# Pads between the four weight tables of a banded attention and feed-forward kernel

## The chip, the cores and the metric

The kernel runs on one core of a Trainium2 chip. The metric is the device time of one execution in microseconds. A core has several engines that run their own instruction streams: TensorE (PE in the profile, its weight loads PEld), VectorE (DVE), ScalarE (ACT), GpSimd (POOL) and SyncE (SP), which here issues DMAs. They work on SBUF, a memory of 128 partitions, and on PSUM, into which TensorE writes its products.

## The reference

Attention over a band of 64 keys, eight heads of 64 in each of eight sequences of 576, and behind it two dense layers with a leaky rectifier between them:

```python
scores = scale * np.matmul(q, k.transpose(0, 1, 3, 2))
mask = (rel >= 0) & (rel < window)          # window = 64
attn = softmax(np.where(mask, scores, -1000000000.0))
x = np.matmul(attn, v)                      # as (4608, 512)
h = x @ w_in                                # (512, 2048)
g = np.maximum(h, 0.0) + alpha * np.minimum(h, 0.0)
return (g @ w_out).astype(np.float32)       # (2048, 512)
```

The weights come as 64-bit numbers; the kernel converts them itself.

## The kernel before

The 4608 rows are 36 tiles of 128, taken in 9 blocks of 4. Attention of a tile leaves x, transposed, as the sum of two float32r tiles: xh, the rounded value, and xl, the rest. Each weight is held as such a sum too, in four tables of 128 partitions: `win_h`, `win_l`, `wout_h`, `wout_l`. They are made in lines 317 to 393, from raw pieces that SyncE fetches. For each block a loop runs over f from 0 to 15 (16 groups of 128 hidden units). A cell (one f of one block) has these steps:

- `hidden` (line 606): h, 128 units by 512 rows, is the sum of 12 products: win_h with xh, win_h with xl, win_l with xh, each over 4 chunks c. The stationary operand, loaded into TensorE ahead of the product, is a 128x128 piece of the weight table, the moving one 512 columns of xh or xl.
- `slopes`, `most`, `high`, `rest` (lines 612 to 630): ScalarE and VectorE apply the rectifier, ScalarE rounds to gh, and GpSimd takes the rest as gl (VectorE in block 0).
- `outs` (line 644): for each of the 4 tiles three products add to the output: gh with wout_h, gh with wout_l, gl with wout_h. Here a 128x128 piece of gh or gl is stationary, and 512 columns of the table move. Output tiles are copied out and stored at f = 15.

In block 0 the first four f are done in two halves of 256 rows.

The tables hold f from 0 to 11. What belongs to f from 12 to 15 lies in rooms of another pool, sb, that loads of q, k and v use first (`LATE`, line 214; `weight`, line 285, finds the place).

TensorE also computes the scores (s, line 466), the transposes of the probabilities (t, line 529, with the tile ident) for the first 8 tiles, their products with v (av, line 565), and idle products (spare, line 304, with one tile as both operands) that fill its waits at the start.

The order of all work is made by a planner in lines 51 to 206: each step is given engines and durations written in the code, 300 random trials with a fixed seed look for a good order, and the instructions are issued in it.

Where a tile lies in SBUF follows from the order in which the pools hand out room. The pool const begins with masks (1024 bytes in a partition), ident (512), alpha_sb (512), three tiles of 64 and six of 32 bytes; then come the four tables, xh and xl (16,384 bytes each) and pt_0. The pool sb comes behind it.

Of the kernel before, what the change touches and what calls it, by code (L numbers as in the profile page):

```python
# [10 lines left out]
F32 = mybir.dt.float32  # L11
# [39 lines left out]
class Plan:  # L51
# [144 lines left out]
    def fill(self, done):  # L196
# [14 lines left out]
NBLK = 4  # L211
PAIRS = 4

LATE = (("wout_h", 12, "z0"), ("wout_h", 14, "z1"), ("wout_l", 12, "z2"), ("wout_l", 14, "z3"),
        ("win_h", 12, "z4"), ("win_h", 14, "z5"), ("win_l", 12, "z6"), ("win_l", 14, "z7"))
ROOMS = {0: ("q", "k", "z0"), 1: ("q", "k", "z1"), 2: ("z4", "z5", "z2"), 3: ("z6", "z7", "z3")}
# [7 lines left out]
def banded_attention_then_prelu_ffn(  # L224
# [12 lines left out]
    P = 128  # L237
# [16 lines left out]
    const = ctx.enter_context(tc.tile_pool(name="const", bufs=1))  # L254
# [21 lines left out]

    stats = [[const.tile([P, NH], F32, name=f"{x}{i}") for x in ("nm", "sm", "rc")] for i in range(2)]


    parts_of = {}  # L280
    for name in ("win_h", "win_l", "wout_h", "wout_l"):
        ends = sorted(f for n, f, _ in LATE if n == name)
        parts_of[name] = {0: const.tile([P, ends[0], E], F32R, name=name)}

    def weight(name, f):
        f0 = max(x for x in parts_of[name] if x <= f)
        return parts_of[name][f0][:, f - f0, :]
# [8 lines left out]
    stock.update({f"x{i}": [i] for i in range(RING)})  # L296
    for _, _, z in LATE:
        stock[z], stock["late " + z] = [z], []
# [18 lines left out]
    def weights(c):  # L317
# [46 lines left out]
        def late(part):  # L364
            return [Buffer("late " + z, 1) for n, f0, z in LATE if (n, f0) == (name + part, f)]

        def begin(part):
            for n, f0, z in LATE:
                if (n, f0) == (name + part, f):
                    f1 = min([x for m, x, _ in LATE if m == n and x > f0], default=NF)  # L370
                    parts_of[n][f0] = sb.tile([P, f1 - f0, E], F32R, tag=z, name=f"{n}_{f0}")
# [365 lines left out]
    for n in range(2, NB + 1):  # L737
        for i in (0, 1):
            m, f = (n - 1, STAYS[1]) if i else (n - 2, STAYS[0]) if n > 2 else (1, 1)
            stays[m, f] = [n * NBLK + 2 * i, n * NBLK + 2 * i + 1] if n < NB else []  # L740
    for n in range(NB):
        ts = list(range(n * NBLK, (n + 1) * NBLK))
        if n < 2:
            for i, t in enumerate(ts):
                if n == 0:
                    _, _, st_done[t] = attend(t, True, EARLY[i])
                else:
                    f = 4 * i - 4 * (i == 3) // 3
# [69 lines left out]
```

## Time and profile before

| what | value |
|---|---|
| median of 3 runs | 896.2 us |
| lowest, highest | 895.82, 896.66 us |
| profiled execution | 895.07 us |
| its span | 893.3 us |
| ScalarE rescaling h (line 612) | 688 ns each |
| GpSimd taking gl (line 629) | 1290 ns each |

The span is the time from the first to the last instruction of the profiled execution; the execution's own time is 1.8 us longer. "Busy" is the time in which an engine has at least one instruction under way. A matmul's duration in the profile reaches from its start to its modelled end, and the next one starts before that end, so the pace of TensorE is read from the distance between starts.

### The profile page before, as it was taken

The page shows a single profiled execution, that of the slowest core. Times are in us where ns is not written, and L with a number is a line of the kernel's source. Part 1 is how long each engine was busy: PE and PEld are TensorE (multiplying, and loading weights), DVE is VectorE, ACT ScalarE, POOL GpSimd, SP SyncE. Part 2 cuts the span into 40 slices and gives each one's busy share as a digit, 9 for nine tenths or more (in the row PEclk, how much of TensorE's full clock was granted, in tenths as well). Part 3 has the DMA queues.
Part 4 walks back from the last instruction along what each step waited for, and adds up shares of the span by engine and source line. Part 5 has one row for each costly group of instructions (what it writes and reads, how often), then busy time and mean ns, then how long its engine had stood idle before and what let it go on. Part 6 is the DMA issues. An engine that isn't in the chain of part 4 may idle for free.

```text
span 893.3 us, 15479 instructions
## 1 busy us (share of the span) xinstructions
PE 885.7 (99%) x5951; PEld 733.9 (82%) x5951; DVE 429.2 (48%) x1319; ACT 380.6 (43%) x1022; POOL 307.6 (34%) x240
## 2 busy tenths in 40 slices
PE   8999999999999999999999999999999999999998
PEld 8888788888888888888888888888888888888886
DVE  6889863762726181716344362627171726311111
ACT  7988755433334262524352433335152524222222
POOL 5777842332313232323131332314142323121221
PEclk9999999999999999999999999999999999999999
DMA  8766643122203050303130212104030311001001
GB/s 308 238 229 192 194 129 107 28 79 51 105 17 91 1 153 2 107 1 107 48 107 1 80 75 51 56 13 142 1 107 1 107 47 49 1 1 48 1 0 49
DMA packets 55387, 69.70 MB, mean 78 GB/s; under 512 B 3456, under 2 KB 48784, under 8 KB 55312
## 3 DMA queue, kind: packets, MB, share of 16 engines
q1 hardware_dynamic: 54576, 68.04, 24.3%
q8 instruction: 47, 0.77, 0.4%
q10 hardware_dynamic: 736, 0.66, 0.2%
q14 instruction: 28, 0.23, 0.1%
HBM read 59.25 MB, written 9.44 MB: 77 GB/s over the span
## 4 chain that ended last, share of the span: by engine, by line
PE 93%; ACT 2%; DMA 2%; DVE 1%; POOL 1%; issue 0%; ACTq 0%; POOLq 0%; SPq 0%; DVEq 0%
PE h L606 43%; PE o L644 42%; PE s L466 4%; PE av L565 4%; DMA raw<-w_out 1%; ACT w L495 1%; DMA q<-qT 1%; POOL val L360 0%; PE t L529 0%; PE spare L304 0%; ACT g L612 0%; DVE val L356 0%; ACT win_h L375 0%; ACT wout_h L375 0%; ACT xh L569 0%
## 5 line engine op out<-in xcount | busy, mean ns | idle before, releaser
L629 POOL TENSOR_TENSOR gl<-g,gh 128x512 fp32r<-128x512 f32 x128 | 165.1, 1290 | 385.2 <-PE o L644 246.1
L619 DVE SCALAR_TENSOR_TENSOR g<-h,s_sb,g 128x512 f32<-128x512 f32 x128 | 96.1, 751 | 292.1 <-ACT g L612 292.0
L644 PE MATMUL o<-wout_h,gh 128*128 128x512 f32 x576 | 225.3, 391 | 0.0
L644 PE MATMUL o<-wout_l,gh 128*128 128x512 f32 x576 | 224.4, 390 | 0.3 <-DVE wout_l L379 0.3
L612 ACT ACTIVATE g<-h,sa_sb 128x512 f32<-128x512 f32 (+1 forms) x148 | 100.1, 676 | 227.2 <-PE h L606 199.8
L495 ACT ACTIVATE w<-w,nm 128x128 f32<-128x128 f32 x288 | 112.2, 393 | 114.0 <-DVE nm L489 113.9
L644 PE MATMUL o<-wout_h,gl 128*128 128x512 f32 x576 | 159.0, 389 | 0.0
L606 PE MATMUL h<-xh,win_h 128*128 128x512 f32 (+1 forms) x592 | 157.7, 388 | 0.6 <-ACT gh L625 0.4
L606 PE MATMUL h<-xl,win_h 128*128 128x512 f32 (+1 forms) x592 | 155.0, 384 | 0.0
L606 PE MATMUL h<-xh,win_l 128*128 128x512 f32 (+1 forms) x592 | 155.0, 384 | 0.0
L550 DVE STREAM_TRANSPOSE pt<-w 32x256 f32<-32x256 f32 x336 | 141.4, 430 | 6.3 <-POOL w L512 2.1
L625 ACT CAST gh<-g 128x512 fp32r<-128x512 f32 x128 | 79.4, 620 | 133.1 <-DVE g L619 83.9
L606 PEld LDWEIGHTS h<-xh,win_h 128*128 128x128 f32 x592 | 108.1, 188 | 24.7 <-issue 2.4
L512 POOL TENSOR_TENSOR w<-w,rc 128x1024 f32<-128x1024 f32 (+1 forms) x44 | 70.1, 1593 | 168.7 <-DVE rc L508 167.9
L606 PEld LDWEIGHTS h<-xl,win_h 128*128 128x128 f32 x592 | 109.5, 188 | 22.2
L606 PEld LDWEIGHTS h<-xh,win_l 128*128 128x128 f32 x592 | 109.5, 188 | 22.2
L644 PEld LDWEIGHTS o<-wout_h,gh 128*128 128x128 f32 x576 | 108.1, 188 | 22.9 <-issue 0.5
L644 PEld LDWEIGHTS o<-wout_l,gh 128*128 128x128 f32 x576 | 108.2, 188 | 22.7 <-DVE wout_l L379 0.6
L644 PEld LDWEIGHTS o<-wout_h,gl 128*128 128x128 f32 x576 | 108.1, 188 | 22.6
L489 DVE CUSTOM_DVE_ANT_0 w<-s,masks 128x128 f32<-128x128 f32 x288 | 63.8, 286 | 123.4 <-PE s L466 123.4
L495 ACT ACTIVATION_READ_ACCUMULATOR w<-w,nm 128x1 f32 x288 | 54.8, 190 | 0.0
L360 POOL TENSOR_TENSOR val<-val,low 128x512 int32<-128x512 int32 x32 | 41.0, 1290 | 11.8 <-DVE val L356 7.5
(52 smaller groups left out, 490.5 us busy)
## 6 DMA issues: line engine op xcount, KB each, us to landing
v<-vN SPq DMA_DIRECT2D x72, 256.0 KB, 4.5
k<-kT SPq DMA_DIRECT2D x35, 384.0 KB, 5.7
out<-os SPq DMA_DIRECT2D x35, 256.0 KB, 2.2
q<-qT SPq DMA_DIRECT2D x34, 256.0 KB, 5.7
raw<-w_in SPq DMA_DIRECT2D x16, 512.0 KB, 4.5
raw<-w_out SPq DMA_DIRECT2D x16, 512.0 KB, 4.2
k<-kT SPq DMA_DIRECT2D x2, 192.0 KB, 3.2
q<-qT ACTq DMA_DIRECT2D x2, 128.0 KB, 3.4
```

What stands on the lines that cost most here:

```text
L360: nc.gpsimd.tensor_tensor(out=d["val"], in0=d["val"], in1=d["tail"], op=ALU.add)
L466: nc.tensor.matmul(some[x][h * W:(h + 1) * W, u, y - ys.start], q[r, y, h, u * W:(u + 1) * W], k[r, y, u:u + 2, h, :], start=True, stop=True)
L489: nc.vector.tensor_tensor_reduce(out=w, in0=s, in1=m, op0=ALU.add, op1=ALU.min, scale=-SCALE, scalar=3.0e38, accum_out=d["nm"][:, g:g + 1])
L495: nc.scalar.activation(w, w, AF.Exp, scale=-1.0, bias=d["nm"][:, g:g + 1], accum_out=d["sm"][:, g:g + 1])
L512: nc.gpsimd.tensor_tensor(out=w, in0=w, in1=d["rc"][:, g].unsqueeze(2).broadcast_to(list(w.shape)), op=ALU.mult)
L550: nc.vector.transpose(d["pt"][ks, :, r], d["w"][r, :, ks])
L606: nc.tensor.matmul(ph[:, :nt], weight(wt, f)[:, c * P:(c + 1) * P], xt[:, c, xs], start=(k == 0), stop=(k == 3 * NP - 1))
L612: nc.scalar.activation(d["g"], d["h"][:, :nt], AF.Copy, scale=sa_sb[:, f:f + 1])
L619: nc.vector.scalar_tensor_tensor(out=g, in0=d["h"][:, :nt], scalar=s_sb[:, f:f + 1], in1=d["g"], op0=ALU.mult, op1=ALU.max)
L625: nc.scalar.copy(d["gh"], d["g"])
L629: (nc.vector if start else nc.gpsimd).tensor_tensor(out=d["gl"], in0=d["g"], in1=d["gh"].bitcast(F32), op=ALU.subtract)
L644: nc.tensor.matmul(po[t], gt[:, i * P:(i + 1) * P], weight(wt, f), start=(f == 0 and k == 0), stop=(f == NF - 1 and k == 2))
```

## The change

Three tiles without use are allocated in the pool const: 16 floats behind win_h, 16 behind win_l and 32 behind wout_h. A float has four bytes, so the pads have 64, 64 and 128 bytes in each partition.

```diff
+SHIFTS = {"win_h": 16, "win_l": 16, "wout_h": 32}
+
...
     parts_of = {}
     for name in ("win_h", "win_l", "wout_h", "wout_l"):
         ends = sorted(f for n, f, _ in LATE if n == name)
         parts_of[name] = {0: const.tile([P, ends[0], E], F32R, name=name)}
+        if name in SHIFTS:
+            const.tile([P, SHIFTS[name]], F32, name=f"pad_{name}")
```

Everything allocated behind a pad is moved by it. Counted within a line of 512 bytes, win_l starts 64 bytes further on than win_h, wout_h 128, and wout_l, xh, xl, pt_0 and the pool sb 256.

## The prediction

> **What bounds the kernel now.** I read the page's busy table first, then its chain, to learn which engine sets the end.
>
> ```profile
> span 893.3 us, 15479 instructions
> PE 885.7 (99%) x5951; PEld 733.9 (82%) x5951; DVE 429.2 (48%) x1319; ACT 380.6 (43%) x1022; POOL 307.6 (34%) x240
> ...
> PE 93%; ACT 2%; DMA 2%; DVE 1%; POOL 1%; issue 0%; ACTq 0%; POOLq 0%; SPq 0%; DVEq 0%
> ```
>
> TensorE is busy 99% of the span, and 93% of the chain that ended last is TensorE work. Matmuls overlap, though, so a busy TensorE can still lose time between two starts. The chain in order of time shows how fast the starts follow each other:
>
> ```profile
> 190.68 10.88 PE h L606 x48
> 201.56 13.60 PE o L644 x60
> ...
> 775.99 13.60 PE o L644 x60
> ```
>
> Each piece is a start, a duration and a count. 10.88 / 48 and 13.60 / 60 are both 0.2267 us: one product with 512 columns every 226.7 ns, for h and for o alike, early and late in the run. Nothing but the product itself sets that pace, as the waits of TensorE show. These are its longest:
>
> ```profile
> PE spare L304 <- DVE xl L303: 1.1, 1, 1.1
> PE s L466 <- DMA q<-qT: 1.1, 1, 1.1
> PE av L565 <- DVE pt L536: 0.5, 1, 0.5
> PE h L606 <- ACT gh L625: 0.4, 1, 0.4
> ```
>
> Three microseconds among them. The throttle is no cause either; the mean clock is in the row of the core:
>
> ```profile
> core 0: 893.3 us, clock 0.999
> ```
>
> Next I ask how much of the 226.7 ns is columns and how much comes once per product. The first four f of block 0 are done in halves of 256 columns; the timeline of TensorE alone has them:
>
> ```profile
> 21.41 0.64 PE L606 MATMUL h<-xl,win_h 128*128 128x256 f32 x4
> 21.89 0.64 PE L606 MATMUL h<-xh,win_l 128*128 128x256 f32 x4
> ```
>
> Four starts from 21.41 to 21.89 are 0.12 us each. So 256 more columns cost 226.7 - 120 = 106.7 ns, which is 0.417 ns a column; 512 columns are 213.3 ns, and 13.3 ns of each product depend on no column count. The page's groups give the number of products:
>
> ```profile
> L644 PE MATMUL o<-wout_h,gh 128*128 128x512 f32 x576 | 225.3, 391 | 0.0
> L644 PE MATMUL o<-wout_l,gh 128*128 128x512 f32 x576 | 224.4, 390 | 0.3 <-DVE wout_l L379 0.3
> ...
> L606 PE MATMUL h<-xh,win_h 128*128 128x512 f32 (+1 forms) x592 | 157.7, 388 | 0.6 <-ACT gh L625 0.4
> ```
>
> There are three groups of 576 for o and three of 592 for h: 3 x 576 + 3 x 592 = 3504 products. The fixed part is 3504 x 13.3 ns = 46.7 us, 5% of the span. **That is all this change could reach**: the columns themselves cannot get cheaper by an address.
>
> **The change part by part.** It adds three tiles that nobody writes or reads. No instruction, DMA or wait is added, removed or moved: the order comes from durations written in the code and a fixed random seed, and neither sees an address. Cost in instructions: zero.
>
> What moves is where tiles start. A table has 12 x 512 x 4 = 24,576 bytes in each partition, 48 lines of 512; xh, xl and every tile of the sb pool are whole lines as well. Before, therefore, both operands of each product in question start at the same place of a line. The pads are 64, 64 and 128 bytes, and all that comes after wout_h is shifted by their sum, 256. Counted by loops (9 blocks of 4 tiles; f below 12 in the tables, f from 12 to 15 in the sb pool, which moves with x and g):
>
> - win_h with xh and xl, 256 apart: 9 x 12 x 8 + 32 (the halves of block 0) = 896 products
> - win_l with xh, 192 apart: 448
> - wout_h with gh and gl, 128 apart: 9 x 12 x 8 = 864
> - wout_l with gh, 0 apart as before: 432
> - all products of f from 12 to 15, 0 apart as before: 9 x 4 x 24 = 864
>
> So 2208 of 3504 get a distance, and 2208 x 13.3 ns = 29.4 us is the most that distance can save.
>
> The trace has no such product at a distance other than 0, so the cost of one is bounded by the nearest rows. From below it is the columns alone: 213.3 ns, fixed part gone. From above there is no row of a product that fetches worse; the nearest is the load of the weights, which runs beside each stream:
>
> ```profile
> L606 PEld LDWEIGHTS h<-xl,win_h 128*128 128x128 f32 x592 | 109.5, 188 | 22.2
> L529 PEld LDWEIGHTS t<-ident,w 128*128 128x128 f32 x64 | 7.2, 140 | 2.1 <-POOL w L512 0.8 <-issue 0.3
> L304 PEld LDWEIGHTS spare<-xl 128*128 128x128 f32 x78 | 10.9, 216 | 1.4 <-DVE xl L303 1.1 <-issue 0.2
> ```
>
> A load takes 188 ns for h, 216 for spare (one tile as both operands, so 0 apart) and 140 for t, the one 128x128 product whose operands already differ: ident starts 1024 bytes behind masks and the tables 2432, so w and ident lie 128 apart in a line. If a bad distance cost h what spare's load takes more, 216 - 188 = 28 ns, the fixed part would be 41.3 ns and 2208 products would lose 62 us. If a good one took off the 48 ns by which t is shorter, the whole 13.3 would be gone. But t differs from h in being a transposition, and spare's mean holds its start-up, so neither is a price. I take 13.3 ns unchanged, the value of the row that it is nearest to: h and o themselves.
>
> Why unchanged, when t speaks the other way? A collision of two reads should vary with who reads. Yet the pace is 226.7 ns in the pieces for h, whose stationary operand is a weight, and for o, whose stationary operand is g, and it is 13.3 ns whether the load falls beside 256 columns or 512. Other traffic does not change it either. The windows give, in turn, the stretch, its length, the busy time of TensorE, its loads, VectorE, ScalarE and GpSimd, then the clock, the DMA share and GB/s:
>
> ```profile
> 0.00:25.00 25.00, 22.59 (x328) 20.34 (x329) 17.12 (x95) 19.61 (x76) 12.83 (x22) 1.00 0.85 291
> 25.00:150.00 125.00, 123.40 (x893) 101.19 (x894) 96.23 (x243) 90.95 (x218) 80.89 (x66) 1.00 0.57 184
> ...
> 600.00:870.00 270.00, 270.00 (x1636) 223.76 (x1631) 100.83 (x297) 93.78 (x237) 74.36 (x54) 1.00 0.14 43
> ```
>
> From 600 to 870 three other engines read and write SBUF for 101, 94 and 74 of 270 us, and the piece at 775.99 still has 226.7 ns per product. A number so even looks like a cost of the product, not of what it meets. That is an argument, no proof: with everything 0 apart, a collision that always falls in the same phase would look as even.
>
> The Trainium skill, page "SBUF — State Buffer", section "Who interferes with whom", goes further: TensorE has one read port for the moving operand and another, independent one for the weights, and it waits on nobody. By that rule distance is worth nothing and the sum is 0; no row here can show ports.
>
> The Trainium skill, page "TensorE: Matmul & The Clock Gate", section "Wait — 56ns, not 53.3ns?", gives the fixed cost of a warm matmul as about 2.5 ns. The rows here have 13.3, so the measurement differs; if distance restored the page's figure, the sum would be an estimated 2208 x 10.8 ns = 24 us less.
>
> The remaining tiles keep their distances among themselves. VectorE, ScalarE and GpSimd see operands shifted by 256 bytes together (masks, ident and the small tables stay). I cost that at nothing: TensorE covers it, since none of the three is busy over half the span. If an operation took 5% more, VectorE would be at 451 us, still covered. DMA landings move by 256 bytes in a line as well, and that is the one place without full cover: before the first h at 20.82 us TensorE stands behind loads, with DMA engines at 0.85. No landing of size at such a place is in the trace; if it made transfers 10% slower (my assumption), 20.82 us would grow by at most 2.1, and if they gained as much it would shrink by as much. I take 0. The row of that start:
>
> ```profile
> 20.82 0.74 PE L606 MATMUL h<-xh,win_h 128*128 128x256 f32 x4
> ```
>
> **The sum.** 0 instructions + 2208 x 0 ns + 0 for landings: the profiled execution, 895.07 us (span 893.3 and 1.8 around it), stays at 895.07. It lies 1.1 us below the median of the runs, 896.2, so the median stays at **896.2**, give or take 1.0 for the spread of the runs and small changes at the start.
>
> **The rivals.**
>
> *Distance ends a collision (faster).* The load of the next weights sweeps the line in which the stream reads, and with equal starts they meet; the 13.3 ns are that meeting. For it: the load of t at 128 apart is the short one, and a fixed part independent of columns is what a meeting once per load gives. Against it: the evenness above. If three quarters go, 2208 x 10 ns = 22 us: 896.2 - 22 = 874. All of it gives 866.8; only the 896 products at 256 apart, at 10 ns, give 887. The other engines would follow, because GpSimd works 1.29 us in the 5.44 us that 24 products take, and VectorE and ScalarE have like slack; late next would be the weights of the first 150 us, where VectorE is busy 96 of 125 us, so part of the gain there would be lost.
>
> *Distance makes a collision (slower).* The stream needs a new column every 0.417 ns, the load is slower, so equal starts may be the phase in which the stream is always ahead. A head start of 128 to 256 bytes for the wrong side then puts it behind the load in each product. For it: all 24 products of a cell are 0 apart and run at one even pace. Against it: nothing in the trace shows a worse phase. If the fixed part doubles, 2208 x 13.3 = 29.4 us and the median is 925.6; it decides against the change from 1.8 us on, that is 0.8 ns per product.
>
> *The change does nothing it says.* If tiles that nobody reads got no room, or all tables were moved alike, distances would stay 0. That gives 896.2 again and counts with the forecast.
>
> **How the numbers follow.** No change has 0.64: evenness over users, columns and traffic, against a confounded row. The faster rival has 0.21, the slower one 0.15 (of which 0.04 is the start alone, 898 at most). About 0.2%, 1.8 us, is what a measurement of this kernel can tell from no change; the cases fall clearly inside or outside, so faster 0.21, same 0.64, slower 0.15. The forecast alone, 895.2 to 897.2, would leave 0.36 out, so the range has to reach one way. It goes down to 869, which takes in the faster rival but for its extreme end, and up to 899 for the start; left out is about 0.15, and the whole bounds of the unknown cost, 866.8 and 958, lie beyond.
>
> **What would show each step.** The chain's piece of 60 o products must last 13.60 us again if distance is nothing; with the faster rival, groups with wout_h get shorter starts than the wout_l group (0 apart) between them, and f from 12 on stays at 226.7 ns, so that the pieces differ inside one run. The slower rival shows the same split the other way. The load rows should stay at 188 ns; 140 would speak for the meeting. The first h should start at 20.8 us; a later start convicts the landings. The prediction is wrong if any two distances show a different pace.

## The result, and the profile after

The changed kernel takes 905.59 us (median of 3 runs, 905.45 to 905.95) against 896.2 before. The ratio is 1.0102, with a 95% interval of 1.0088 to 1.0115: **about 1% slower**, beyond the upper end of the predicted range.

From the page of the changed kernel, first the span and the busy table, then the groups of the six products and one of their loads (busy us and mean ns of one behind the bar):

```profile
span 903.9 us, 15479 instructions
PE 896.3 (99%) x5951; PEld 734.7 (81%) x5951; DVE 429.6 (48%) x1319; ACT 380.0 (42%) x1022; POOL 307.9 (34%) x240
...
L647 PE MATMUL o<-wout_h,gh 128*128 128x512 f32 x576 | 226.7, 394 | 0.0
L647 PE MATMUL o<-wout_l,gh 128*128 128x512 f32 x576 | 225.8, 392 | 0.3 <-DVE wout_l L382 0.3
...
L647 PE MATMUL o<-wout_h,gl 128*128 128x512 f32 x576 | 160.7, 391 | 0.0
L609 PE MATMUL h<-xh,win_h 128*128 128x512 f32 (+1 forms) x592 | 159.2, 390 | 1.0 <-ACT two L340 0.4
L609 PE MATMUL h<-xh,win_l 128*128 128x512 f32 (+1 forms) x592 | 157.4, 388 | 0.0
L609 PE MATMUL h<-xl,win_h 128*128 128x512 f32 (+1 forms) x592 | 155.9, 385 | 0.0
...
L609 PEld LDWEIGHTS h<-xl,win_h 128*128 128x128 f32 x592 | 109.5, 188 | 23.7
```

The program has the same 15479 instructions, VectorE, ScalarE and GpSimd are busy as long as before, and a load still takes 188 ns. TensorE is busy 10.6 us longer, and the span is 10.6 us longer. The wout_l products, still 0 apart, have also become longer (390 to 392 ns): the loss isn't confined to the products with a new distance.

Two pieces of the chain in order of time, where 48 products took 10.88 us and 60 took 13.60 before:

```profile
192.72 11.00 PE h L609 x48
203.72 13.76 PE o L647 x60
```

One cell of f below 12 late in the run, in the timeline of TensorE (start, duration to the last modelled end, count):

```profile
836.77 1.09 PE L609 MATMUL h<-xh,win_h 128*128 128x512 f32 x4
837.70 1.09 PE L609 MATMUL h<-xl,win_h 128*128 128x512 f32 x4
838.62 1.09 PE L609 MATMUL h<-xh,win_l 128*128 128x512 f32 x4
839.55 0.39 PE L647 MATMUL o<-wout_h,gh 128*128 128x512 f32 x1
...
841.39 1.08 PE L647 MATMUL o<-wout_h,gl 128*128 128x512 f32 x4
842.31 0.40 PE L609 MATMUL h<-xh,win_h 128*128 128x512 f32 x1
```

From start to start the 24 products take 842.31 - 836.77 = 5.54 us; 24 x 0.2267 were 5.44. So this cell loses 0.10 us. If all 108 cells (12 f in 9 blocks) lost as much, that would be 10.8 us, an estimate from one cell, and about the whole difference. The last cells of the same run, f = 14 and 15, have their weights in the sb pool, 0 apart:

```profile
886.53 1.07 PE L609 MATMUL h<-xh,win_h 128*128 128x512 f32 x4
887.44 1.07 PE L609 MATMUL h<-xl,win_h 128*128 128x512 f32 x4
888.35 1.07 PE L609 MATMUL h<-xh,win_l 128*128 128x512 f32 x4
889.25 1.07 PE L609 MATMUL h<-xh,win_h 128*128 128x512 f32 x4
```

Here twelve products take 889.25 - 886.53 = 2.72 us, 226.7 ns each, as before. The early weights pay, the late ones don't. The start is innocent, as the timeline of the changed kernel shows (the first h began at 20.82 us before):

```profile
20.67 0.74 PE L609 MATMUL h<-xh,win_h 128*128 128x256 f32 x4
```

### The profile page after: what moved, and what is told of

It reads as the page before. It is cut to its first block, busy times and chain, and to the rows that moved or that the text cites. A ratio compares the mean times of both kernels' runs of the same rounds, so it can differ in the third digit from the quotient of the medians.

```text
span 903.9 us, 15479 instructions
## 1 busy us (share of the span) xinstructions
PE 896.3 (99%) x5951; PEld 734.7 (81%) x5951; DVE 429.6 (48%) x1319; ACT 380.0 (42%) x1022; POOL 307.9 (34%) x240
## 4 chain that ended last, share of the span: by engine, by line
PE 92%; ACT 3%; DMA 3%; DVE 1%; issue 1%; POOL 0%; ACTq 0%; DVEq 0%; SPq 0%
PE h L609 42%; PE o L647 42%; PE s L469 4%; PE av L568 3%; DMA raw<-w_out 2%; ACT w L498 1%; DMA q<-qT 1%; ACT two L340 1%; DMA raw<-w_in 1%; PE t L532 0%; PE spare L307 0%; ACT low L355 0%; ACT pt L537 0%; ACT win_h L378 0%; ACT g L615 0%
## 5 line engine op out<-in xcount | busy, mean ns | idle before, releaser
L647 PE MATMUL o<-wout_h,gh 128*128 128x512 f32 x576 | 226.7, 394 | 0.0
L609 PE MATMUL h<-xh,win_l 128*128 128x512 f32 (+1 forms) x592 | 157.4, 388 | 0.0
```

The source lines that it names most:

```text
L609: nc.tensor.matmul(ph[:, :nt], weight(wt, f)[:, c * P:(c + 1) * P], xt[:, c, xs], start=(k == 0), stop=(k == 3 * NP - 1))
L647: nc.tensor.matmul(po[t], gt[:, i * P:(i + 1) * P], weight(wt, f), start=(f == 0 and k == 0), stop=(f == NF - 1 and k == 2))
```

## The experiments

The questions were which distances cost, whether a product pays for its own distance or for a change between neighbours, and why products at 0 apart pay too.

**Streams of products alone.** A kernel with two tiles, W (stationary) and X (moving), in streams of 60 products; the numbers are the starts in bytes.

```diff
+SEGMENTS = [
+    ('dist64b', (64,), (0,), 128, 512, False),
...
+    ('alt16b', (0, 16), (0,), 128, 512, False),
...
+            nc.tensor.matmul(acc[0:cols, 0:n], (Wb if half else W)[:, a:a + cols], (Xb if half else X)[:, b:b + n],
...
```

> This kernel computes none of the reference: it runs streams of 60 float32r products each, with the start of the stationary and of the moving operand set per stream, and writes q's first rows to the output. Theory A (a change of distance costs): a product pays for its distance only when it differs from that of the products before it. Every stream of constant distance, 0 to 384 bytes, settles after some 10 products at 226.7 ns between starts; the streams that alternate between two distances stay between 229 and 232; a switch every 12 lies between. Theory B (the distance itself costs): constant streams differ for good: 0 at 226.7, 192 and 128 at 230 to 233, 256 at 230; an alternating stream has the mean of its two constant ones, about 228 to 229. Theory C (the place in the line, not the distance): moving both operands together by 128 bytes costs as much as moving one. For the fixed part of 13.3 ns: if it comes with the load, a stationary operand of 64 columns has about half of it (220 ns), of 32 a quarter (217); if it is a cost of the product, both stay at 226.7.

The timeline of TensorE in this kernel, one row per stream:

```profile
21.02 13.76 PE L60 MATMUL dist0b<-X,W 128*128 128x512 f32 x60
34.62 13.77 PE L60 MATMUL dist16b<-X,W 128*128 128x512 f32 x60
48.23 14.15 PE L60 MATMUL dist32b<-X,W 128*128 128x512 f32 x60
62.23 14.16 PE L60 MATMUL dist64b<-X,W 128*128 128x512 f32 x60
76.22 14.11 PE L60 MATMUL dist128b<-X,W 128*128 128x512 f32 x60
90.17 13.90 PE L60 MATMUL dist192b<-X,W 128*128 128x512 f32 x60
103.91 13.77 PE L60 MATMUL dist256b<-X,W 128*128 128x512 f32 x60
117.51 14.11 PE L60 MATMUL dist384b<-X,W 128*128 128x512 f32 x60
131.46 13.96 PE L60 MATMUL alt16b<-X,W 128*128 128x512 f32 x60
145.25 14.12 PE L60 MATMUL alt64b<-X,W 128*128 128x512 f32 x60
```

The distance between two starts, over 60, is the pace: 13.60 us or 226.7 ns at 0 and 256; 14.00 or 233.3 at 32 and 64; 13.95 or 232.5 at 128 and 384; 13.74 or 229.0 at 192. These streams have no change inside, so theory A as stated falls: **a constant distance can cost for good**, and it repeats after 256 bytes. But theory B isn't enough: 16 costs nothing alone (226.8), yet alternating between 0 and 16 takes 13.79 / 60 = 229.8 ns. Streams in groups show the same: changing between 0 and 192 after every four products took 230.0 ns, more than either distance alone, and after every twelve 227.5. Theory C fell between: moving both operands together by 128, product by product, took 228.4, less than the 232.3 of moving W alone and the 230.0 of moving X alone.

The expectation about the fixed part failed on both sides: with 64 stationary columns the stream took 230.0 ns, with 32 columns 231.7, *more* than with 128. The prediction's split of a product held, though: a stream of products with 256 columns took 7.20 us, 120.0 ns each, as in block 0 of the kernel.

**One distance of 256 for all early products.** One pad behind wout_l:

```diff
+PADS = {'wout_l': 256}
...
+        if name in PADS:
+            const.tile([P, PADS[name] // 4], F32, name=f"pad_{name}")
```

> One pad of 256 bytes behind wout_l: all four tables start at the same place of a line, and x, g and the late tables 256 further. Every product of f below 12 is 256 apart, those from 12 on 0 apart, so the distance changes only twice a block. Theory A: 896 to 898 us, as before but for some ten products after each of 18 changes (18 x 10 x 4 ns = 0.7 us). Theory B: the win_h products of the changed kernel, 256 apart, took about 230 ns; 2640 products with 3.5 ns more each are 9 us, so about 905.

Measured: 896.08 us, ratio 0.9993 (0.9983 to 1.0002). No loss. Alone this looks like theory A, but as 256 equals 0 in the streams, it follows from the distance as well; the run didn't tell the theories apart.

**One table moved at a time.** win_l, wout_h and, further below, win_h are each allocated further up among the small tiles, in a kernel of its own, so that it alone gets the distance that it has in the changed kernel. For win_l:

```diff
     sa_sb = const.tile([P, NF], F32, name="sa_sb")
+    moved = {"win_l": const.tile([P, 12, 512], F32R, name="win_l")}
...
```

For wout_h the tile stands behind the first two of the six tiles of 32 bytes.

> Only win_l is moved (by 320 bytes in a line, 192 apart from xh); everything else stays 0 apart. Theory A: two changes of distance in each of 108 cells of f below 12, so the four win_l products and several behind them lose, some 50 to 60 ns a cell: 108 x 0.055 = 6 us more than before, about 902. Theory B: the 448 products of win_l alone lose 5.6 ns each, 2.5 us: 898.7.

> Only wout_h is moved, to 128 apart from gh and gl as in the changed kernel; everything else stays 0 apart. Theory A: in o the distance changes at every product, 36 ns lost per cell of f below 12 and a tail in the h behind it of 10 to 30: 108 x 0.046 to 0.066 = 5 to 7 us, 901 to 903. Theory B: 864 products lose 3.5 ns each, 3.0 us: 899.2.

Measured: win_l alone 902.04 (ratio 1.0054, 1.0035 to 1.0074), wout_h alone 901.99 (1.0051, 1.0032 to 1.0071). Both are 5.6 to 5.7 us above the 896.38 of the kernel before in the same runs. By the ratios it is 4.6 to 4.8 us (2.9 to 6.6). For win_l that is about twice theory B's sum. A cell with win_l alone moved shows why, in the timeline:

```profile
823.58 1.07 PE L608 MATMUL h<-xh,win_h 128*128 128x512 f32 x4
824.49 1.07 PE L608 MATMUL h<-xl,win_h 128*128 128x512 f32 x4
825.39 1.09 PE L608 MATMUL h<-xh,win_l 128*128 128x512 f32 x4
826.32 0.39 PE L646 MATMUL o<-wout_h,gh 128*128 128x512 f32 x1
...
828.17 1.07 PE L646 MATMUL o<-wout_h,gl 128*128 128x512 f32 x4
```

The four win_l products take 0.93 us instead of 0.907. The eight products of o behind them are 0 apart and still take 828.17 - 826.32 = 1.85 us instead of 1.81. **The loss has a tail** in products that are themselves well placed. With wout_h alone moved:

```profile
825.35 0.40 PE L648 MATMUL o<-wout_h,gh 128*128 128x512 f32 x1
825.58 0.39 PE L648 MATMUL o<-wout_l,gh 128*128 128x512 f32 x1
...
827.19 1.09 PE L648 MATMUL o<-wout_h,gl 128*128 128x512 f32 x4
828.11 1.08 PE L610 MATMUL h<-xh,win_h 128*128 128x512 f32 x4
829.03 1.07 PE L610 MATMUL h<-xl,win_h 128*128 128x512 f32 x4
```

The first eight take 1.84 us, the four with gl 0.92, and even the four of the next h 0.92; only then is the pace back.

**Distances in steps of 16, each behind products at 0.** This asks for the settling itself (theory D) against a price without memory (E). It is the stream kernel with other segments.

```diff
...
+    ('back64b', (0,), (0,), 24),
+    ('dist64b', (64,), (0,), 60),
+    ('back80b', (0,), (0,), 24),
...
```

> Computes none of the reference: streams of float32r products as before, now each stream of 60 at one distance, in steps of 16 bytes, comes behind 24 products at distance 0. Distance here is how far the stationary operand's start lies behind the moving one's in a line; in the mov streams the moving one is moved instead, so mov192 should equal dist64, mov64 equal dist192, and both64 and both128 equal 0, if only the difference counts. Theory A (only a change costs) has fallen with the first such kernel: constant 64 stayed at 233.3, constant 128 at 232.5. Theory D (settling): only near distance 0, with a period of 256 bytes, do the products settle at 226.7; at any other distance they stay unsettled at 228 to 234, and on the return to 0 the first 7 to 10 products still lose, some 20 to 30 ns together. Theory E (price without memory): the same price by distance, but the first product back at distance 0 is at 226.7 at once. A distance that is better than 0 would show below 226.7; neither expects one.

Its timeline:

```profile
69.08 5.60 PE L70 MATMUL back64b<-X,W 128*128 128x512 f32 x24
74.52 14.16 PE L70 MATMUL dist64b<-X,W 128*128 128x512 f32 x60
88.52 5.64 PE L70 MATMUL back80b<-X,W 128*128 128x512 f32 x24
94.00 14.07 PE L70 MATMUL dist80b<-X,W 128*128 128x512 f32 x60
...
171.72 13.76 PE L70 MATMUL dist144b<-X,W 128*128 128x512 f32 x60
185.32 5.61 PE L70 MATMUL back160b<-X,W 128*128 128x512 f32 x24
...
345.23 14.16 PE L70 MATMUL mov192b<-X,W 128*128 128x512 f32 x60
359.23 5.62 PE L70 MATMUL backmov192b<-X,W 128*128 128x512 f32 x24
```

After 60 products at 64, the 24 at 0 take 94.00 - 88.52 = 5.48 us; the 24 before dist64b (they come after 48) take 5.44. Most of the lost 0.04 us lies in the first seven products, which came 231, 231, 235, 229, 232, 231 and 227 ns apart; then they stayed at 226.7 up to the last, beside which the next distance is loaded already. So theory E falls: **the pace has a memory**, up to some ten products long. Theory D holds with two corrections. What the return costs depends on where the stream comes from: 0.04 to 0.05 us from 64, 112, 160 or 208, at most 0.01 us from the other distances that W was given. And 144 and 240 settle too, at 13.60 us; all other multiples of 16 that were tried, but 0 and 16, stayed at 228.9 to 234.2 ns. Moving X by 192 equals moving W by 64 (14.00 us each), as a difference should; moving both by 64 or 128 settled at 226.7 after a tail. No distance was faster than 0.

**One distance of 128 for all early products.** `PADS = {'wout_l': 128}`:

> One pad of 128 bytes behind wout_l: all 2640 products of f below 12 are 128 apart, without a change between neighbours. Theory A (only a change costs): 896 to 898. Theories D and E (128 does not settle): 2640 x (232.5 - 226.7 = 5.8 ns) = 15.3 us more, 911 to 912, slower than the changed kernel though it has one distance only.

Measured: 912.11, ratio 1.0182 (1.0167 to 1.0197), 15.9 us more. One pad without any change between neighbours costs more than the changed kernel's three. That settles it against theory A in the kernel itself.

**win_h alone, and the changed kernel without win_l's part.**

For win_h alone:

```diff
     flip_sb = const.tile([P, NF], I32, name="flip_sb")
+    moved = {"win_h": const.tile([P, 12, 512], F32R, name="win_h")}
```

> Only win_h is moved, 256 apart from xh and xl; all else 0 apart. Theories D and E (256 counts as 0): 896.4, no change. Theory B of the first runs (256 costs some 3.5 ns in 896 products): 899.5.

For the changed kernel with win_l back:

```diff
+PADS = {'win_l': 128, 'wout_h': 128}
```

> The changed kernel with win_l put back beside win_h (pads of 128 behind win_l and behind wout_h): h is 256 apart throughout, o as in the changed kernel. Theory D: what is left is wout_h and its tails, as with wout_h alone: 901.5 to 902.5. Theory E: 864 products at 5.8 ns, 5.0 us: 901.4. If the gain by putting win_l back is 3 to 4 us, less than the 5.7 that win_l cost alone, the two tables share their tails.

Measured: win_h alone 896.15, ratio 1.0 (0.9987 to 1.0014), no change. With win_l put back 901.96, ratio 1.0071 (1.0054 to 1.0088), as with wout_h alone. So in the changed kernel win_l costs 905.59 - 901.96 = 3.6 us by the medians, against 5.7 alone. That its tail runs into o, which loses anyway, would explain the difference, but it isn't shown: by the intervals of the ratios win_l alone may have cost as little as 3.1 us.

**16 bytes, where a stream settles.** The table, first of the four in the pool, gets 8 floats more and starts 4 floats inside; all that comes behind it is moved by 32 bytes together.

```diff
...
+            whole = const.tile([P, ends[0] * E + 8], F32R, name=name)
+            parts_of[name] = {0: whole[:, 4:4 + ends[0] * E].rearrange("p (f e) -> p f e", e=E)}
...
```

> win_h starts 16 bytes ahead of xh and xl in a line (a distance at which a constant stream settles at 226.7), all else is 0 apart. The distance changes twice in each cell of f below 12, between two distances that both settle. If only unsettled products and the return from them cost: 896.2, no change, since the streams that went from 16 to 0 and from 240 to 0 lost nothing. If every change of distance costs a tail, whatever the distances: 20 to 30 ns twice a cell, 108 x 0.05 = 5 us, 901.

> wout_h starts 16 bytes ahead of gh and gl in a line, all else is 0 apart. In o the first eight products of a cell alternate between 16 and 0. Each distance settles alone, but the stream that alternated between them stayed at 229.9: 108 cells x 8 x 3.2 ns = 2.8 us more, 899, and up to 4 with tails. If the distance alone sets the price: 896.2.

Measured: win_h 896.59, ratio 1.0006 (0.9996 to 1.0016): changes between two settled distances are free there. wout_h 902.35, ratio 1.0073 (1.0058 to 1.0088): both expectations missed. A cell of its timeline:

```profile
825.34 0.40 PE L650 MATMUL o<-wout_h,gh 128*128 128x512 f32 x1
...
827.18 1.10 PE L650 MATMUL o<-wout_h,gl 128*128 128x512 f32 x4
828.12 1.07 PE L612 MATMUL h<-xh,win_h 128*128 128x512 f32 x4
829.02 1.07 PE L612 MATMUL h<-xl,win_h 128*128 128x512 f32 x4
```

The eight products with gh take 1.84 us and the four with gl 0.94: start by start, the wout_h products come at 233 ns and the wout_l products between them at 227. The four of the next h take 0.90, so there is no tail. wout_h is the moving operand of o, while in the stream that settled at 16 the stationary one was moved; hence the last run, with X moved in steps of 16.

> Computes none of the reference: streams of 60 float32r products behind 24 at distance 0 again, but now the moving operand's start goes from 16 to 240 in steps of 16 bytes while the stationary one stays at 0 of a line; in the both streams the two move together (distance 0). It asks what the 233 ns of wout_h at 16 bytes are. Theory F (a moving operand whose start is no multiple of 32 pays 6.7 ns by its place): both16 and both48 stay at 233.3 although the distance is 0, and mov16, mov112, mov240 are at 233. Theory G (distance alone): both16, both32 and both48 settle at 226.7, and so do mov16, mov112 and mov240, which have the distances of the settled streams 240, 144 and 16; mov64, mov128 and mov192 as before at 229, 233 and 233.

Its timeline:

```profile
288.69 14.16 PE L74 MATMUL mov240b<-X,W 128*128 128x512 f32 x60
302.69 5.60 PE L74 MATMUL backboth16b<-X,W 128*128 128x512 f32 x24
308.12 13.96 PE L74 MATMUL both16b<-X,W 128*128 128x512 f32 x60
321.93 5.63 PE L74 MATMUL backboth32b<-X,W 128*128 128x512 f32 x24
327.40 13.80 PE L74 MATMUL both32b<-X,W 128*128 128x512 f32 x60
341.03 5.63 PE L74 MATMUL backboth48b<-X,W 128*128 128x512 f32 x24
```

Both operands moved by 16, 0 apart, take 13.81 us or 230.2 ns and don't settle; moved by 32 they take 13.63 with a tail at the head, and end at 226.7. So G falls, the place of the moving operand counts beside the distance; F has its direction, but the price was 3.5 to 4.5 ns (both16, both48), not 6.7. None of the 15 places tried for X with W at 0 settled (229.2 to 234.7 ns). One of them is the case of wout_h: in mov240 the moving operand also starts 16 bytes ahead of the stationary one and at no multiple of 32. It took 14.00 us, 233.3 ns a product, and the 24 products behind it lost nothing (5.43 us), just as in the kernel. How place and distance together make these 233 ns stays open.

## Why the prediction was wrong

- **What bounds the kernel**: right. The change could act only through the pace of 3504 products, and it did, by 10.6 us of span. The instructions stayed the same, TensorE's idle time stayed at 7.6 us (span less busy time, before and after), a load stayed at 188 ns, the other engines' busy times stayed, and the landings did no harm.
- **Which products get a distance**: the count was right, but the prediction counted places within a line of 512 bytes, an assumption; in the streams the pace repeats after 256. So 896 of the 2208 (win_h, 256 apart) are as good as 0 apart and cost nothing, as win_h alone shows. What pays are the 448 of win_l, the 864 of wout_h, and, by the tails, products at 0 apart.
- **The step that failed** is the value taken for the unknown cost: "I take 13.3 ns unchanged", the term 2208 x 0 ns of the sum, with the reason that an even number "looks like a cost of the product, not of what it meets". In its place 9.4 us were measured: by the streams 6.6 ns for each product of win_l, 6.5 for each of wout_h and none for win_h, and tails behind them. The evenness came from a state into which the stream settles while both operands keep a favourable distance; it said nothing of other distances. The prediction saw this hole ("a collision that always falls in the same phase would look as even") and gave it too little weight. With every product of the trace at the same distance, the trace couldn't measure what the change varied.
- **The slower rival** had the direction right: equal starts are among the best places, and no distance tried was faster. Its mechanism, that the stream falls behind the load, wasn't measured, and its price was off. It doubled the fixed part in 2208 products, 29.4 us. The streams give 6.6 ns for win_l (its 192 from the moving side is their 64, 256 less 192) and 6.5 for wout_h (mov128, 13.99 us): an estimate of 448 x 6.6 + 864 x 6.5 = 8.6 us without tails, where 9.4 were measured.
- **The faster rival** is refuted for the distances tried, multiples of 16 bytes: 13.3 ns is the least fixed part that any float32r stream showed. The short load of t was no hint of a good distance; the loads of h stayed at 188 ns in every kernel with moved tables.
- **What would show it**: the split inside one run came, f of 12 and above back at 226.7. The split between wout_h and wout_l was blurred by the tail, which the prediction had not thought of.

The Trainium skill, page "SBUF — State Buffer", section "Who interferes with whom", has TensorE's two read ports independent and TensorE waiting on nobody. What the prediction drew from it, that distance is worth nothing, the streams here contradict: with no other engine at work, the two operands' starts alone changed the pace from 226.7 to 234.2. No run shows ports, and whether the reads collide anywhere wasn't measured; "settling" describes what the starts do, and its cause stays open.

## What to carry to other kernels

If a profile has only one value of what a change varies, an even pace is no sign that the pace doesn't depend on it: bound it from both sides and let the range show that. For streams of float32r products, let the tables that serve as operands start at the same place within 256 bytes and keep the moving operand on a multiple of 32, and let a small tile or a pad never shift one of them alone; here that was worth 1 to 2% of a kernel bound by TensorE (905.59 and 912.11 against 896.2 us). When a loss shows in products that were not touched, look at what ran up to ten products earlier.

## What the runs showed of the hardware

- With 512 columns, float32r products came every 226.7 ns at the best places and up to 234.7 at others (mov208 in the last run), with a period of 256 bytes (226.7 at 0 and 256, 232.5 at 128 and 384).
- The pace has a memory: behind stationary operands at 64, 112, 160 or 208 bytes, the first products back at 0 still lost 0.03 to 0.05 us together, over some six to eight products; behind the other distances tried for the stationary operand at most 0.01.
- With both operands moved together by 32, 64 or 128 bytes the pace settled at 226.7 ns; moved by 16 or 48 it stayed at 230.2 and 231.2.
- Fewer stationary columns made it worse, though their loads are shorter (134 and 109 ns against 188): 230.0 ns with 64 columns, 231.7 with 32, against 226.7 with 128, all at distance 0.
- bf16 products in the first stream kernel came every 216 ns, the same with starts that alternate by 128 bytes. That agrees with the 215.7 ns of the Trainium skill, page "TensorE: Matmul & The Clock Gate", section "Wait — 56ns, not 53.3ns?"; the fixed part of float32r, 13.3 ns, is beyond what that section gives.
